# A spectral layer on 32x64 tokens with X(k) and X(-k) side by side, and an FFN on normalised rows in 64-row PE tiles

## The chip, the cores and the metric

The kernel runs on one core of one Trainium2 chip. The metric is the time of one execution on the device in microseconds (us), lower is better. A time quoted for a kernel is the median of its runs. The span that a profile shows is the time from the first to the last instruction on the core; it is 1.6 to 2.8 us shorter than the time of the same run in the runs here. Engines are written PE (matrix multiplications), PEld (loading of weights for PE), DVE (vector engine), ACT (scalar engine), POOL, and SP, which here only issues DMAs. A DMA is carried out by 16 DMA engines in packets, the contiguous pieces that the trace records one by one.

## The reference, cut to what matters

The reference applies the same two kinds of layers twice, first A, then B, then A, then B, with the same weights both times. The input has 2048 tokens with 448 features in bf16.

```
def _A_ref(x, w_r, w_i):                       # spectral layer
    X = rfft2(x.astype(float32), axes=(-2, -1))      # 2048 x 225
    X = X * (w_r + 1j * w_i)
    return irfft2(X, s=(S, D)).astype(bfloat16)

def _B_ref(x, w1, b1, w2, b2):                 # FFN: 448 -> 1792 -> 448
    h = einsum("bsd,df->bsf", x, w1) + b1
    r = where(h > 0, h, 0)
    return einsum("bsf,fd->bsd", r * r, w2) + b2

x = A_x
x = x + _A_ref(_layernorm(x), A_w_r, A_w_i)
x = x + _B_ref(_layernorm(x), B_w1, B_b1, B_w2, B_b2)
x = x + _A_ref(_layernorm(x), A_w_r, A_w_i)
x = x + _B_ref(_layernorm(x), B_w1, B_b1, B_w2, B_b2)
```

The complex weights W = w_r + i w_i have 2048 x 225 elements each for the real and the imaginary part. One row, without its first column, is 224 elements, which is 448 bytes in bf16.

## The kernel before

The transform over the 2048 tokens is done in two factors, 16 x 128. The names of the stages, which the profile lets one tell apart by their tiles, are these:

- A: a 16-point transform over token tiles (weights `Fs`).
- TD (layer 1) or TQ (layer 2): the transform over the features (tiles `TD_sb` and `TQ_sb`).
- B: the 128-point transform over the tokens (`G_sb`).
- W: DVE multiplies by the spectral weights.
- Bi: the 128-point inverse (`H_sb`, `HS_sb`).
- TI and AI: the inverse over the features and the last 16 points (`TI_sb`, `FI_sb`), which form the ramp into the FFN.
- h and o: the two products of the FFN, both with `W_sb`.

A real input gives X(k) and X(-k) that belong together, so each block needs the weights of row k and of row -k. The kernel loads both halves of W with all 128 partitions as destination, each row once, and makes the mirrored order of the second half with PE and a permutation matrix J:

```
w_dram = [w.rearrange("(p k) l -> p k l", k=16) for w in (A_w_r, A_w_i)]
for i in range(2):
    dma("sp", Wn[:, i, :, :], w_dram[i][:, 9:16, 1:225])        # 128 partitions
...
    dma("sp", Wp[:, :, 2 * i, :], w_dram[i][:, 1:8, 1:225])     # 128 partitions
...
def w_mirror(p):
    q = _Tile(1)
    for i in range(2):
        mm(q[...], J_sb[:], Wn[:, 1 - i, 7 - p, :], i == 0, i == 1, skip=True)
    evac(Wp[:, p - 1, 1:4:2, :], q[...], EV["M"])
```

The first product of the FFN contracts over 448 features. The kernel pads them to four blocks of 128 rows. The rows are not normalised; the spare rows of the fourth block carry sums of columns of W1 and the bias, with which the mean is corrected, and the factor of the normalisation is applied at the end, in `o_tile`:

```
def h_part(c, fb, t0, t1):
    ...
    for blk in range(4):                       # 4 full passes for 3.5 blocks of features
        mm(q[...], W1_sb[:, blk, fb * P:(fb + 1) * P], yT[:, 4 * c + t0:4 * c + t1, blk, :],
           blk == 0, blk == 3)
    act(hb, q[...], ACT.Relu)
    tt(hb, hb, hb, ALU.mult)
```

A list scheduler in the program fixes the order of all instructions on every engine when the kernel is built. It works from assumed costs and from priorities that stand in a table. In the profile nearly every matmul bears the line of one helper (L530), so groups are told apart by tile names and shapes.

Of the kernel before, what the change touches and what calls it, by code (L numbers as in the profile page):

```python
# [10 lines left out]
P = 128  # L11
S = 2048
# [10 lines left out]
SD_PAIRS = (4, 5, 6, 7)  # L23
H_PAIRS = tuple(p for p in range(1, 8) if p not in SD_PAIRS)

# [9 lines left out]
def make_constants():  # L35
# [3 lines left out]
    comp = np.zeros((16, 16))  # L39
    hi = np.arange(16)  # L40
    comp[0] = 1.0
    comp[1] = np.cos(np.pi * hi)
    for p in range(1, 8):
        comp[2 * p] = np.cos(2 * np.pi * p * hi / 16)
        comp[2 * p + 1] = -np.sin(2 * np.pi * p * hi / 16)
    FA = np.zeros((16, 8, 16, 8))
    for j in range(8):
        FA[:, j, :, j] = comp.T
# [24 lines left out]
    m = np.arange(P)  # L73
    lo = (m % 8) * 16 + m // 8
    k2 = np.arange(P)
    kk = [0, 8, 1, 2, 3, 4, 5, 6, 7]
    G = np.zeros((P, 9, 3, P))
    H = np.zeros((P, 9, 2, 2 * P))
    for i, k1 in enumerate(kk):
        th = 2 * np.pi * lo[:, None] * (k1 + 16 * k2[None, :]) / float(S)  # L80
        G[:, i, 0] = np.cos(th)
        G[:, i, 1] = -np.sin(th)
        G[:, i, 2] = np.sin(th)
        hr = np.cos(th).T
        hm = np.sin(th).T
        if i < 2:
            H[:, i, 0] = np.concatenate([hr, hm], 1)
            H[:, i, 1] = np.concatenate([-hm, hr], 1)
        else:
            a = np.stack([hr.reshape(P, 16, 8), hm.reshape(P, 16, 8)], 2)  # L90
            b = np.stack([-hm.reshape(P, 16, 8), hr.reshape(P, 16, 8)], 2)
            H[:, i, 0] = a.reshape(P, 2 * P)
            H[:, i, 1] = b.reshape(P, 2 * P)
# [9 lines left out]

    HS = np.stack([np.stack([-H[:, p + 1, 1], H[:, p + 1, 0], H[:, p + 1, 1], -H[:, p + 1, 0]], 1) for p in SD_PAIRS], 1)
    H = H[:, [0, 1] + [p + 1 for p in H_PAIRS]]
    return dict(HS=HS, FA=np.concatenate([FA, -FA], 1), FI=np.concatenate([FI, -FI], 1), TD=TD, G=G, H=H, TI=TI, TQ=TQ,
# [4 lines left out]
PR = {'A1': 65800.0, 'A1step': 7500.0, 'TD': [48800.0, -113100.0], 'B': [36300.0, -23900.0], 'W': [76300.0, 35800.0], 'Bi': [21700.0, 28400.0], 'step': [16400.0, 1100.0], 'M': 33500.0, 'aux': -104400.0, 'ramp': [210200.0, 192900.0], 'rstep': [2800.0, 6700.0], 'late': [85200.0, 100700.0], 'lstep': [5400.0, 6200.0], 'TI': [53500.0, 42800.0], 'AI': [44600.0, 400.0], 'h': [57700.0, -6500.0], 'A2': -27100.0, 'xb': 113100.0}  # L111
LOOK = {'act': 0.0, 'dve': 50.0, 'pe': 0.0}
EV = {'A1': ['act'], 'A2': ['act'], 'TD': ['act', 'dve'], 'B': ['act', 'dve'], 'Bi': ['act', 'dve'], 'Bi0': ['act', 'dve'], 'TI': ['act'], 'M': ['act', 'dve'], 'T': ['act', 'dve'], 'XR': ['pool'], 'FS': ['pool'], 'FS2': ['dve']}
SPLIT = (1, 2, 4)
NFLIP = 2
HALVES = True
# [3 lines left out]
class _Op:  # L120
    __slots__ = ("eng", "fn", "deps", "has_dep", "ticket", "is_dma", "dsem", "cost", "lat", "unit", "gdeps", "alt")

    def __init__(self, eng, fn, is_dma, cost, lat):
        self.eng = eng
        self.fn = fn
        self.deps = []
        self.gdeps = []
        self.has_dep = False
        self.ticket = None
        self.is_dma = is_dma  # L130
        self.dsem = None
        self.cost = cost
        self.lat = lat
        self.unit = None
        self.alt = None

# [6 lines left out]
class _Unit:  # L143


    def __init__(self, eng, tile=None):
        self.eng = eng
        self.ops = []
        self.tile = tile
        self.prio = 0.0  # L150
        self.bias = 0.0
        self.seq = 0

# [29 lines left out]
def _pages(ap):  # L183

    if isinstance(ap, _PsAP):
        return [ap.tile]
# [7 lines left out]
    return [(name, int(i)) for i in pg]  # L194


class _Sched:
# [6 lines left out]
    DMA_RATE = 400.0  # L204

    def __init__(self):
# [5 lines left out]
        self.look = dict.fromkeys(self.ENGINES, 0.0)  # L212
        self.warm_fn = None
# [3 lines left out]
        self.warm_share = 0.45  # L217

    def add(self, eng, fn, reads=(), writes=(), is_dma=False, cost=100.0, lat=130.0, unit=None):
# [24 lines left out]
        elif tile is not None and tile.unit is not None:  # L244
            u = tile.unit
        else:
            u = _Unit(eng, tile)
            u.bias = self.bias
            u.seq = len(self.units)
            self.units.append(u)  # L250
            if tile is not None:
                tile.unit = u
# [3 lines left out]
        op.unit = u  # L256
        u.ops.append(op)
        return op

    def schedule(self):  # L260
# [17 lines left out]
        for u in self.units:  # L278
            if u.tile is not None:
                for r in u.tile.readers:  # L280
                    for d in r.gdeps:
                        if d.unit.seq < u.seq:
                            order[d.unit].add(u)
                            npred[u].add(d.unit)
        free = {e: 0.0 for e in self.ENGINES}
# [8 lines left out]

        def enter(u):
            for e in u.ops[0].alt or (u.eng,):
                cand[e].append(u)

        for u in self.units:
            if left[u] == 0:  # L300
                enter(u)
        ready = {}

        def ready_of(u):
            if u not in ready:
                r, off = 0.0, 0.0
                for op in u.ops:
                    for d in op.gdeps:
                        if d.unit is not u:
                            same = d.eng == u.eng and not d.is_dma  # L310
                            r = max(r, done[d] + d.lat + (80.0 if u.eng == "pe" else 0.0) - off)
                    off += op.cost
                ready[u] = r
            return ready[u]
# [11 lines left out]

        total = len(self.units)
        while total:
            choice = None
            for e in self.ENGINES:  # L330
                avail, starts = {}, []
                for u in cand[e]:
                    r = ready_of(u)
                    if u.tile is not None:
                        if u.tile.n not in avail:
                            avail[u.tile.n] = pick_banks(u.tile.n, free[e])
                        if avail[u.tile.n] is None:
                            continue
                        r = max(r, avail[u.tile.n][0])
                    starts.append((max(r, free[e]), u))  # L340
                if starts:

                    t0 = min(s for s, u in starts) + self.look[e]
                    best = min(((-u.prio, u.seq, s, u) for s, u in starts if s <= t0), key=lambda k: k[:2])
                    key = (best[2], best[0], best[1])
                    if choice is None or key < choice[0]:
                        choice = (key, best[3], e)
            assert choice is not None, "no unit can run"
            start, u, e = choice[0][0], choice[1], choice[2]
            if e == "pe":  # L350

                while self.warm_fn is not None:
                    gap = start - free["pe"]
                    recent = sum(min(b, free["pe"]) - max(a, free["pe"] - 3400.0) for a, b in used[-60:]
                                 if b > free["pe"] - 3400.0)
                    cold = free["pe"] < self.cold_until
                    unit = 430.0 if cold else 216.0
                    if gap < unit + (150.0 if cold or recent < self.warm_share * 3400.0 else 700.0):
# [16 lines left out]
                if u.tile is not None and start < free["pe"]:  # L375
                    start = free["pe"]
            for a in u.ops[0].alt or (e,):
                cand[a].remove(u)
            if u.ops[0].alt:
# [4 lines left out]
            if u.tile is not None:  # L384
                b = pick_banks(u.tile.n, start)[1]
                u.tile.bank = b
                for i in range(b, b + u.tile.n):
                    old = bank_user[i]
                    if old is not None and old is not u.tile:
# [3 lines left out]
                    bank_user[i] = u.tile  # L393
            t = start
            for op in u.ops:
                t += op.cost
# [5 lines left out]
                for a in (op.gdeps if e != "pe" else ()):  # L402
                    if a.eng == "pe" and a.unit.tile is not None:
                        for i in range(a.unit.tile.bank, a.unit.tile.bank + a.unit.tile.n):
# [44 lines left out]
def bass_interleave_layers__spectral_gfnet__dense_activation_squared_relu__prompt_kernel(nc, A_x, A_w_r, A_w_i, B_x, B_w1, B_b1, B_w2, B_b2, out):  # L449
# [6 lines left out]
    with ExitStack() as es:  # L456
# [7 lines left out]
        x_sb = sb("x_sb", [P, NT, 4 * P])  # L464
        xin = sb("xin", [P, NT, D])
        XA = sb("XA", [P, 2, 2, 16, P])
# [3 lines left out]
        Z = arena[:, 7168 * 2:7168 * 2 + 32 * 256].rearrange("p (c l) -> p c l", c=32)  # L470
# [4 lines left out]
        VT = sb("VT", [P, 2, 2, NT, 16, 8])  # L475
# [3 lines left out]
        Wn = yT[:].rearrange("p a b c -> p (a b c)")[:, 0:2 * 7 * LW].rearrange("p (r k l) -> p r k l", r=2, k=7)  # L479
        Wt = sb("Wt", [P, 32, LW])  # L480
        TD_sb = sb("TD_sb", [P, 2, 2, LW])
        G_sb = sb("G_sb", [P, 9, 3, P])
        H_sb = sb("H_sb", [P, 2 + len(H_PAIRS), 2, 2 * P])
        HS_sb = sb("HS_sb", [P, len(SD_PAIRS), 4, 2 * P])
# [8 lines left out]
        W1_sb = sb("W1_sb", [P, 4, FF])  # L493
        W2_sb = sb("W2_sb", [P, FB, D])
# [4 lines left out]
        r2 = rstd[:, :, 4:8]  # L499
# [13 lines left out]
        def dma(eng, o, i, transpose=False):  # L513
            reads = [i] if i.tensor.name in onchip else []
            writes = [o] if o.tensor.name in onchip else []
# [6 lines left out]
            else:  # L522
# [3 lines left out]
                sch.add(eng, fn, reads, writes, is_dma=True, cost=60.0 if eng == "sp" else 100.0,  # L526
                        lat=2.0 * n / sch.DMA_RATE)

        def mm(o, lhsT, rhs, start, stop, skip=False):
# [603 lines left out]
```

## Time and profile before

The first three runs had a median of 291.64 us (288.81 to 291.81). With the fourth run, made beside the changed kernel, the median is 290.23 us.

These are the lines of part 1 (busy time), part 2 (the span in 40 slices) and part 4 (the chain of waits by engine) of the page of the kernel before. In part 2 a digit is the busy share of a slice in tenths; PEclk is the clock granted to PE in tenths; a slice is 7.15 us.

```profile
PE 270.9 (95%) x1769; PEld 163.6 (57%) x1771; DVE 210.4 (74%) x738; ACT 175.4 (61%) x375; POOL 13.3 (5%) x28
...
PE   7799999799999999999996989889999999999996
...
PEclk9999999999999999999999999999999999999999
DMA  7999400010321000110000000020221300020001
GB/s 259 337 376 373 100 0 1 21 19 2 73 40 38 0 0 2 37 38 2 0 0 2 0 1 2 0 40 0 71 71 37 76 32 32 0 71 32 0 18 48
...
PE 81%; DVE 13%; DMA 2%; issue 1%; ACT 1%; POOL 1%; SPq 0%; DVEq 0%; POOLq 0%
```

PE is busy for 95% of the span, never at a reduced clock, and the chain that ended last goes through PE for 81% of its length. DMA is busy mainly in the first five slices (later digits are at most 3).

These are lines of part 5, the groups of instructions: line, engine, operation, tiles, shapes, count, then busy us and mean ns of one, then idle time before them and what ended it.

```profile
L530 PE MATMUL ps<-yT,W_sb 128*128 128x512 bf16 (+1 forms) x560 | 98.6, 337 | 1.3 <-ACT VT L913 0.7
L549 ACT ACTIVATE arena<-ps 128x512 bf16<-128x512 f32 (+1 forms) x140 | 69.3, 514 | 43.4 <-PE ps L530 41.3
```

The first line is the h product: 560 full passes, 98.6 us. The second is its Relu.

The table of stretches gives for each stage its length, the busy time of PE, PEld, DVE, ACT and POOL with the number of instructions, the clock, the busy share of the DMA engines (it is the time of all packet records over 16 engines, so it passes 1 where more than 16 packets are under way at once) and GB/s. The stages were cut where the timeline of PE shows a new tile. The four rows are spectral layer 1, FFN 1, spectral layer 2 and FFN 2.

```profile
19.22:46.45 27.23, 26.19 (x183) 17.19 (x183) 23.86 (x55) 23.12 (x40) 0.00 (x0) 1.00 0.47 152
...
54.02:150.40 96.38, 96.38 (x600) 55.71 (x600) 80.94 (x332) 56.16 (x132) 0.00 (x0) 1.00 0.10 20
...
154.53:180.51 25.98, 24.31 (x164) 15.17 (x166) 21.52 (x49) 21.31 (x35) 0.00 (x0) 1.00 0.00 1
...
188.28:286.00 97.72, 94.33 (x558) 53.43 (x558) 55.86 (x185) 46.42 (x105) 0.00 (x0) 1.00 0.16 39
```

The FFNs are bound by PE alone. The spectral layers are nearly balanced between PE, DVE and ACT. The same table in 4 us steps shows what the DMA engines moved at the start of spectral layer 1:

```profile
20.00:24.00 4.00, 4.00 (x37) 3.26 (x35) 3.50 (x9) 3.20 (x6) 0.00 (x0) 1.00 1.05 343
24.00:28.00 4.00, 4.00 (x32) 2.81 (x29) 3.97 (x12) 3.82 (x8) 0.00 (x0) 1.00 1.06 377
```

Here the queue holds the rest of the weights and constants, and 343 to 377 GB/s go through at a full DMA share while PE is busy all the time. The timeline of PE shows one 512-column chunk of h in FFN 1 (start, length, engine, tiles, count):

```profile
123.88 12.25 PE L530 MATMUL ps<-yT,W_sb 128*128 128x512 bf16 x56
```

### The profile page before, as it was taken

The numbers are of one execution on the slowest core, as the hardware profiler recorded it, in microseconds if no ns is written. First come the engines' busy times: TensorE is split into PE (matmuls) and PEld (weight loads), VectorE is DVE, ScalarE is ACT, GpSimd is POOL, SyncE is SP. The second block draws the span as 40 slices with busy tenths as digits, with TensorE's granted clock in tenths as the row PEclk, the third lists the DMA queues.
The fourth block names the chain that finished last, engine by engine and source line by source line (L and its number), as shares of the span: only waits on it lengthen the run. The fifth ranks groups of instructions, "written<-read, shape, count | busy, mean of one in ns | idle before, by whom it ended". The sixth has DMA issues, their size and how long they took to land.

```text
span 286.0 us, 5056 instructions
## 1 busy us (share of the span) xinstructions
PE 270.9 (95%) x1769; PEld 163.6 (57%) x1771; DVE 210.4 (74%) x738; ACT 175.4 (61%) x375; POOL 13.3 (5%) x28
## 2 busy tenths in 40 slices
PE   7799999799999999999996989889999999999996
PEld 2697746687544455544575554767754454454454
DVE  4959995998998469995695898599589723553432
ACT  2698977998466745347326997796649603623610
POOL 4930000000000000000000000000000000000000
PEclk9999999999999999999999999999999999999999
DMA  7999400010321000110000000020221300020001
GB/s 259 337 376 373 100 0 1 21 19 2 73 40 38 0 0 2 37 38 2 0 0 2 0 1 2 0 40 0 71 71 37 76 32 32 0 71 32 0 18 48
DMA packets 26156, 16.11 MB, mean 56 GB/s; under 512 B 19954, under 2 KB 24786, under 8 KB 26004
## 3 DMA queue, kind: packets, MB, share of 16 engines
q1 hardware_dynamic: 25700, 15.04, 18.8%
q10 hardware_dynamic: 432, 0.75, 0.8%
q8 instruction: 14, 0.23, 0.3%
q14 instruction: 10, 0.08, 0.1%
HBM read 10.29 MB, written 1.84 MB: 42 GB/s over the span
## 4 chain that ended last, share of the span: by engine, by line
PE 81%; DVE 13%; DMA 2%; issue 1%; ACT 1%; POOL 1%; SPq 0%; DVEq 0%; POOLq 0%
PE ps L530 81%; DVE tmp L574 6%; DMA xin<-in_A_x_dram 2%; DVE arena L574 1%; DVE x_sb L889 1%; DVE yT L556 1%; POOL VT L556 1%; DVE x_sb L961 1%; DVE VT L556 1%; DVE st L674 0%; DVE VT L574 0%; DVE arena L556 0%; ACT XA L555 0%; ACT arena L555 0%; ACT VT L913 0%
## 5 line engine op out<-in xcount | busy, mean ns | idle before, releaser
L530 PE MATMUL ps<-yT,W_sb 128*128 128x512 bf16 (+1 forms) x560 | 98.6, 337 | 1.3 <-ACT VT L913 0.7
L549 ACT ACTIVATE arena<-ps 128x512 bf16<-128x512 f32 (+1 forms) x140 | 69.3, 514 | 43.4 <-PE ps L530 41.3
L530 PE MATMUL ps<-W_sb,arena 128*128 128x448 bf16 (+1 forms) x476 | 88.1, 341 | 0.0
L530 PEld LDWEIGHTS ps<-yT,W_sb 128*128 128x128 bf16 x560 | 54.2, 98 | 44.1 <-issue 0.9
L574 DVE TENSOR_TENSOR arena<-arena 128x512 bf16<-128x512 bf16 (+1 forms) x140 | 50.4, 370 | 27.8 <-ACT arena L549 25.0
L530 PEld LDWEIGHTS ps<-W_sb,arena 128*128 128x128 bf16 x476 | 46.0, 98 | 35.6
L961 DVE SCALAR_TENSOR_TENSOR x_sb<-ps,rstd,arena 128x448 bf16<-128x448 f32 (+1 forms) x34 | 22.2, 654 | 26.0 <-PE ps L530 25.8
L555 ACT ACTIVATE arena<-ps 128x896 bf16<-128x896 f32 (+1 forms) x36 | 25.0, 759 | 3.2 <-PE ps L530 2.7
L549 ACT ACTIVATE mv<-mv,epst 128x2 f32<-128x2 f32 (+1 forms) x38 | 10.9, 296 | 23.1 <-DVE mv L675 18.1
L913 ACT ACTIVATE VT<-x_sb 128x448 bf16<-128x448 bf16 x32 | 18.2, 569 | 8.1 <-DVE x_sb L889 7.5
L555 ACT ACTIVATE XA<-ps 128x512 bf16<-128x512 f32 x32 | 17.6, 600 | 7.7 <-PE ps L530 7.6
L555 ACT ACTIVATE VT<-ps 128x512 bf16<-128x512 f32 (+1 forms) x32 | 17.5, 582 | 5.3 <-PE ps L530 5.1
L555 ACT ACTIVATE tmp<-ps 128x896 bf16<-128x896 f32 (+1 forms) x18 | 14.7, 829 | 4.5 <-PE ps L530 4.5
L574 DVE TENSOR_TENSOR tmp<-tmp,Wt 128x896 bf16<-128x896 bf16 (+1 forms) x32 | 16.0, 567 | 0.0
L530 PE MATMUL ps<-HS_sb,arena 128*128 128x512 bf16 x62 | 14.2, 379 | 0.6 <-DVE arena L574 0.4
L530 PE MATMUL ps<-arena,G_sb 128*128 128x448 bf16 (+1 forms) x72 | 14.1, 334 | 0.4 <-ACT arena L555 0.3
L530 PE MATMUL ps<-TI_sb,VT 112*128 112x112 bf16 (+1 forms) x128 | 10.1, 224 | 2.3 <-ACT tmp L555 0.9
L889 DVE SCALAR_TENSOR_TENSOR x_sb<-ps,x_sb 128x448 bf16<-128x448 f32 x16 | 9.6, 622 | 2.9 <-PE ps L530 2.7
L674 DVE BATCH_NORM_STATS2 st<-xin 128x6 f32<-128x448 bf16 x16 | 9.5, 606 | 2.5 <-DMA xin<-in_A_x_dram 2.5
L530 PEld LDWEIGHTS ps<-TI_sb,VT 112*128 112x128 bf16 x128 | 8.3, 97 | 4.4 <-DVE VT L556 1.4
L530 PEld LDWEIGHTS ps<-HS_sb,arena 128*128 128x128 bf16 x64 | 5.9, 98 | 8.3 <-DVE arena L574 1.7
L674 DVE BATCH_NORM_STATS2 st<-x_sb 128x6 f32<-128x448 bf16 (+1 forms) x17 | 10.1, 597 | 0.2
(73 smaller groups left out, 279.4 us busy)
## 6 DMA issues: line engine op xcount, KB each, us to landing
out_dram<-x_sb SPq DMA_DIRECT2D x15, 112.0 KB, 1.7
W_sb<-in_B_w_dram SPq DMA_DIRECT2D x1, 1568.0 KB, 14.4
W_sb<-in_B_w_dram SPq DMA_DIRECT2D x1, 1344.0 KB, 10.1
HS_sb<-c_HS SPq DMA_DIRECT2D x1, 1024.0 KB, 6.0
xin<-in_A_x_dram SPq DMA_DIRECT2D x2, 448.0 KB, 6.0
G_sb<-c_G SPq DMA_DIRECT2D x1, 672.0 KB
xin<-in_A_x_dram ACTq DMA_DIRECT2D x1, 448.0 KB, 5.3
yT<-in_A_w_r_dram SPq DMA_DIRECT2D x1, 392.0 KB, 8.4
```

Of the source, the lines that this page charges most:

```text
L530: sch.add("pe", lambda e: e.matmul(_res(o), lhsT, rhs, start=start, stop=stop, skip_group_check=skip), [lhsT, rhs], [o], cost=max(_free(rh ...
L549: sch.add("act", lambda e: e.activation(o, _res(i), func, **kw), rd, [o], cost=c)
L555: op = sch.add(engs[0], lambda e: e.activation(o, _res(i), ACT.Copy) if h[0].eng == "act" else e.tensor_copy(o, _res(i)), [i], [o], cost=c ...
L556: e.tensor_copy(o, _res(i)), [i], [o], cost=c[engs[0]], unit=unit)
L574: sch.add(eng, lambda e: e.tensor_tensor(o, _res(a), b, op), [a, b], [o], cost=_free(o) / rate + 69.0)
L674: small(lambda e, si=si, xi=xi: e.bn_stats(si, xi), [xi], [si], _free(xi) / 0.96 + 69.0)
L889: small(lambda e, xx=xx, xi=xi, r=r, i=i: e.scalar_tensor_tensor(out=xx, in0=_res(r), scalar=1.0, in1=xi, op0=ALU.mult, op1=ALU.add, accum ...
L913: sch.add("act", lambda e, i=i, o=o, x=x: e.activation(o, x, ACT.Square, accum_out=sd[:, i, 1:2]), [x], [o, sd[:, i, 1:2]], cost=560.0)
L961: small(lambda e: e.scalar_tensor_tensor(out=o, in0=_res(i), scalar=r2[:, t, 0:1], in1=xb[:, t, d0:d1], op0=ALU.mult, op1=ALU.add), [i, r2 ...
```

## The change

Four things are changed together.

1. The token transform is split 32 x 64. A block p then has X(k) and X(-k) side by side in the columns of one tile, the real parts in partitions 0 to 63 and the imaginary parts in partitions 64 to 127. The sums that the mirror needed are now plain column ranges, and Bi costs fewer columns. In exchange W is needed in two arrangements: once with w_r in partitions 0 to 63 and w_i in 64 to 127 (`Was`, in the buffer `x_sb`, in layer 2 in `xin`), and once exchanged (`Wb`, in the buffer `yT`). The rows for -k come from a copy of the second half of W that is reversed in DRAM (`Wrev`).
2. The rows are normalised before the FFN, so only 448 rows of features remain, with no correction rows. The h product runs in 64-row tiles of PE: two half passes on the lower and the upper 64 rows side by side, 7 half passes per feature block in place of 4 full ones. Relu takes the bias as an operand.
3. The mirrors and the corrections go.
4. Every stage and block has its own priority in the scheduler.

The core of the diff, with cuts marked:

```
-        Wn = yT[:]...   Wt = sb("Wt", [P, 32, LW])
-        G_sb = sb("G_sb", [P, 9, 3, P])
-        H_sb = sb("H_sb", [P, 2 + len(H_PAIRS), 2, 2 * P])
-        HS_sb = sb("HS_sb", [P, len(SD_PAIRS), 4, 2 * P])
+        G_sb = sb("G_sb", [P, NP, 2, 192])            # NP = 16
+        H_sb = sb("H_sb", [P, NP, 2, 256])
...
+        Wrev = [nc.dram_tensor(f"Wrev{i}", (16, 64, LW), BF16, kind="Internal").ap() for i in range(2)]
+        for i in range(2):
+            dma("sp", Wrev[i], (A_w_r, A_w_i)[i].rearrange("(q k) l -> k q l", k=32)[16:32, ::-1, 1:225], ...)
...
-        for i in range(2):
-            dma("sp", Wn[:, i, :, :], w_dram[i][:, 9:16, 1:225])
-        ...
+        def load_W(W, f, p0, p1):
+            for i in range(2):
+                rows, w = slice(64 * (i ^ f), 64 * (i ^ f) + 64), w_dram[i]
+                dma("sp", W[rows, p0:p1, 0, :], w[:, p0:p1, 1:225])
+                if p0 == 0:
+                    dma("sp", W[rows, 0:1, 1, :], w[:, 16:17, 1:225])
+            for i in range(2):
+                rows = slice(64 * (i ^ f), 64 * (i ^ f) + 64)
+                r, p = Wrev[i].rearrange("k r l -> r k l"), max(p0, 1)
+                dma("sp", W[rows, p:p1, 1, :], r[:, 16 - p:16 - p1:-1, :], reads=[f"Wrev{i}"])
+        for p0, p1 in RANGES:                          # (0, 4), (4, 10), (10, 16)
+            dma("sp", G_sb[:, p0:p1], dc["G"][:, p0:p1])
+            load_W(Was[0], 0, p0, p1)
+            load_W(Wb, 1, p0, p1)
+            dma("sp", H_sb[:, p0:p1], dc["H"][:, p0:p1])
...
-        def h_part(c, fb, t0, t1):    ... for blk in range(4): mm(... W1_sb[:, blk, ...] ...)
+            def both(u, *runs):
+                for n in range(len(runs[0][2])):
+                    for k, rows, blks in runs:
+                        ... mm(qs[k][...], W1_sb[rows, blk, f], y[rows, :, blk, :], ..., half=True, unit=u)
+            ...
+                both(u, (2 * m, LO, (0, 1, 2, 3)), (2 * m + 1, UP, (0, 1, 2, 3)))
+                    both(u, (2 * j + 1, LO, (0, 1, 3)), (2 * j, UP, (0, 2, 3)))
```

## The prediction

The sum came to -18.8 us (-5 - 3.5 - 12.3 + 2.5 - 0.5, "about -19"). Terms are cut from the text, where marked: the +2.5, the middle of an allowance of 2 to 3 us for about 20 changes between row tiles and full passes, and a named risk that goes with it. The allowance was the author's guess; no run had shown such a cost. It is still contained in the 272.0 us, in the "about -19" and in the lengths given for the FFNs.

> **What bounds it now.** The page shows PE busy 270.9 of 286.0 us (95%), PEclk 9 in every slice; the chain of waits is 81% PE, 13% DVE. Stages by the timeline of PE: start to 9.3; first A to 19.2; spectral layer 1 to 46.5; ramp to 54.0; FFN 1 to 150.4; gap to 154.5; spectral layer 2 to 180.5; ramp to 188.3; FFN 2. The table of stretches shows PE busy all 96.4 us of FFN 1 and 94.3 of 97.7 us of FFN 2. The spectral layers are nearly balanced: layer 1 (27.2 us) PE 26.2, DVE 23.9, ACT 23.1; layer 2 (26.0 us) PE 24.3, DVE 21.5, ACT 21.3; there the chain goes through DVE's multiplications by W.
>
> **What changes, costed from the trace.** In dense runs PE starts a 512-column matmul every 216-218 ns, 256 every 109, 224 about 95, 128 (A2) about 56, 112 (TI) about 50.
> 1. FFN h: 448 rows cost 4 passes now (560 matmuls, 98.6 us). With 64-row tiles they cost 7 half passes, paired, so 3.5: -12.3 us if two row tiles really run together. [...] Relu now takes a bias operand (perhaps 90 ns more on ACT: one-element sqrts take 294 ns with bias, 203 without), but 596+90 stays under PE's new 756 ns a block.
> 2. Inverse stage (Bi): 24,576 columns a layer become 16,384 (18,432 in layer 2), as 128 or 144 matmuls of 128 columns: 10.4 us to about 7.1 and 8.0. B keeps its columns (6.1 us). Mirrors (14 matmuls of 224, 1.3 us) and the sums for the weight correction (16 of 448, 3.0 us) go.
> 3. DVE: the W stage shrinks from about 19 us a layer to 16.8 and 15.7 (four 896-column operations of 535 ns per two blocks); 7 mirror evictions (about 0.56 each) go. Normalising adds 32 tensor_scalars, perhaps 0.35 each; corrections of similar size go.
> 4. DMA: W needs twice the bytes in layer 1 (3.7 MB), reversed through DRAM (0.9 MB), again 3.7 MB for layer 2, under FFN 1. At the 340-375 GB/s of the first slices layer 1's 11 MB land by 31-33 us, in order of need: tight, not binding.
>
> **Sum.** Layer 1: PE needs 19.4 us, DVE and ACT about 20 each, so 27.2 becomes 22 (-5). Layer 2: -3.5. FFNs: -12.3[...]. First A stage: -0.5. Ramps: 0. About -19 in all, nearly all on the critical path.
>
> **Predicted 272.0 us, 263 to 280** (8 in 10). Faster by over 2%: 0.94; within 2%: 0.045; slower: 0.015.
>
> **What would show it.** PE busy near 250; h matmuls in pairs, starts a pair about 216-220 ns apart, 10.6 us instead of 12.1 for a 512-column chunk; Bi about 56 ns a matmul; PEclk still 9; FFN 1 near 91 us, FFN 2 near 92; spectral layers near 22; no waits of DVE on W's DMA over 1 us.
>
> **What would make it wrong.** Row tiles overlapping less than 1.75 times (h then gains nothing); weight loads limiting 64-row pairs at 256 columns or Bi at 128; runs of four columns slowing writes to PSUM in Bi, as layer 2's stride-2 outputs seem to (about 98 ns for 112 columns); [...]W's DMA late in layer 1.

## The result, and the profile after

The changed kernel takes 278.65 us (276.85 to 279.06, four runs) against 290.23 us, and its outputs are correct. A ratio is the mean time of one kernel's fast runs over that of the other's in the same rounds, so it is not quite the ratio of the medians: it is 0.9598, with a 95% interval of 0.9539 to 0.9657. The change is 4% faster. The prediction said 6.7% faster (272.0 of 291.64) with a range of 263 to 280, so the sign and the range hold, while most of the expected gain of some 19 us is there and a part of it isn't.

The same parts of the page, now of the changed kernel (a slice is 6.92 us):

```profile
PE 257.8 (93%) x2385; PEld 168.5 (61%) x2385; DVE 206.8 (75%) x686; ACT 176.5 (64%) x366; POOL 9.6 (3%) x23
...
PE   6699586999998999999999999899999999999995
...
PEclk9999978999999999999999999999999999999999
DMA  7969999702223424202240400002332700111001
GB/s 239 307 143 267 295 244 335 253 2 47 62 48 68 86 40 100 60 0 56 53 93 3 98 2 4 0 2 41 21 75 58 144 3 4 46 50 36 0 22 46
...
PE 67%; ACT 7%; DVE 7%; DMA 1%; issue 1%; DVEq 0%; ACTq 0%
```

In slices 3 to 7 the digits of DMA are as full as before or fuller (6 to 9), yet GB/s is 143, 267, 295, 244, 335 where the kernel before had 376, 373 and was nearly done. In slices 5 to 7 PE is busy only 5, 8 and 6 tenths, and in slices 6 and 7 its clock is reduced. The two groups of the FFN:

```profile
L600 ACT ACTIVATE arena<-ps,b1T 128x512 bf16<-128x512 f32 (+1 forms) x140 | 73.5, 611 | 30.8 <-PE ps L577 30.6
L577 PE MATMUL ps<-yT,W_sb 64*128 64x512 bf16 (+1 forms) x980 | 86.1, 333 | 1.2 <-DMA yT<-xin 0.8
```

The h product fell from 98.6 to 86.1 us of busy time. Here are the four stages again from the table of stretches, in the same order:

```profile
20.07:52.26 32.19, 25.26 (x264) 22.55 (x265) 19.96 (x38) 20.54 (x30) 0.00 (x0) 0.89 1.10 292
...
60.34:150.70 90.36, 89.53 (x785) 51.83 (x785) 83.25 (x325) 57.04 (x133) 0.00 (x0) 1.00 0.27 55
...
154.61:177.25 22.64, 21.56 (x275) 20.39 (x276) 18.31 (x35) 19.97 (x31) 0.00 (x0) 1.00 0.04 9
...
185.84:276.80 90.96, 87.77 (x748) 50.03 (x748) 55.76 (x179) 45.64 (x101) 0.00 (x0) 1.00 0.19 42
```

FFN 1, FFN 2 and spectral layer 2 are 6.0, 6.8 and 3.3 us shorter. Spectral layer 1 is 5.0 us longer, at a granted clock of 0.89 and a DMA share above 1 for its whole length. Laid beside the prediction, in us:

| stage | before | predicted | after | difference after - before |
|---|---|---|---|---|
| start to first TD | 19.2 | 18.7 | 20.1 | +0.9 |
| spectral layer 1 | 27.2 | 22 | 32.2 | +5.0 |
| ramp 1 | 7.6 | 7.6 | 8.1 | +0.5 |
| FFN 1 | 96.4 | 91 | 90.4 | -6.0 |
| gap (FFN 1 to layer 2) | 4.1 | 4.1 | 3.9 | -0.2 |
| spectral layer 2 | 26.0 | 22.5 | 22.6 | -3.3 |
| ramp 2 | 7.8 | 7.8 | 8.6 | +0.8 |
| FFN 2 | 97.7 | 92 | 91.0 | -6.8 |
| span | 286.0 | about 267 | 276.8 | -9.2 |

(The column of predictions is read from the text of the prediction; its parts add to 266. The span of 286.0 belongs to one of the fastest runs of the kernel before, 288.8 us, so the spans differ by 9.2 us and the medians by 11.6.)

Without spectral layer 1 the stages were predicted to give 14 us and gave 14.2. Layer 1 was to give 5 and cost 5. The whole miss of about 10 us lies there. The timeline of PE in this stage shows how the time was lost:

```profile
29.35 2.46 PE L577 MATMUL ps<-TD_sb,XA 128*128 128x224 bf16 x24
35.46 4.14 PE L577 MATMUL ps<-arena,G_sb 128*128 128x224 bf16 x24 [3.65 <-DMA G_sb<-c_G]
39.43 2.84 PE L577 MATMUL ps<-H_sb,arena 128*128 128x128 bf16 x48
42.11 1.46 PE L1104 MATMUL ps<-ones 128*128 128x512 bf16 x6
45.54 0.23 PE L577 MATMUL ps<-H_sb,arena 128*128 128x128 bf16 x1 [1.97 <-DVE arena L635]
46.07 5.30 PE L577 MATMUL ps<-H_sb,arena 128*128 128x128 bf16 x63 [0.30 <-DVE arena L635]
```

PE waits 3.65 us for the last part of G. After this pause the 24 matmuls of 224 columns take 4.14 us, while 24 of the same width (first line) take 2.46. The granted clock is 0.50 from 35.8 us on for 3.4 us (0.60 in the mean from 36 to 40 us, see the table below). Later PE waits only 1.97 us for DVE, and from 46.1 us the clock is again 0.50 for 3.4 us, so that the last 63 matmuls take 5.30 us (3.69 in e12 below). A pause of 2.54 us in e11 below brought no such fall. So in these runs the shorter pause of 1.97 us was followed by a reduced clock and the longer one of 2.54 us was not; what decides it is not shown. The `ones` matmuls are fillers that the scheduler puts where it expects PE to idle. The table of waits says what DVE and PE waited for on DMAs (us in total, times, longest):

```profile
DVE tmp L635 <- DMA yT<-Wrev: 5.8, 2, 2.9
...
PE ps L577 <- DMA G_sb<-c_G: 4.2, 2, 3.6
...
DVE tmp L635 <- DMA x_sb<-Wrev: 2.2, 2, 1.4
```

So 8.0 us of waits of DVE and 4.2 us of PE are on W and G. The table of stretches in 4 us steps:

```profile
20.00:24.00 4.00, 3.93 (x42) 3.96 (x43) 2.06 (x5) 2.56 (x4) 0.00 (x0) 1.00 1.01 291
24.00:28.00 4.00, 3.45 (x39) 3.20 (x37) 2.87 (x7) 3.52 (x6) 0.00 (x0) 1.00 1.21 229
28.00:32.00 4.00, 3.81 (x46) 3.56 (x43) 0.77 (x2) 3.83 (x7) 0.00 (x0) 1.00 1.09 286
32.00:36.00 4.00, 0.54 (x5) 0.53 (x6) 4.00 (x8) 0.89 (x2) 0.00 (x0) 0.98 1.12 285
36.00:40.00 4.00, 4.00 (x32) 3.38 (x31) 2.46 (x5) 2.20 (x3) 0.00 (x0) 0.60 1.20 235
```

The DMA engines are busy all the time and move 229 to 291 GB/s, where the kernel before had moved 343 and 377. Before 20 us they were not even busy: the timeline of SP shows that issuing a W DMA takes about 0.62 us, for 28 KB and for 168 KB alike when nothing else holds SP up, and SP issues them one by one (two in each line). Parts of G, which go to 128 partitions in large packets, took 0.43 us here, the parts of H that follow W 0.68 to 0.72, so the number of partitions alone doesn't decide it. Lines of that timeline:

```profile
12.34 1.25 SPq L572 DMA_DIRECT2D x_sb<-Wrev  x2
13.63 1.27 SPq L572 DMA_DIRECT2D yT<-in_A_w_r_dram  x2
14.94 1.25 SPq L572 DMA_DIRECT2D yT<-in_A_w_i_dram  x2
```

From 12 to 16 and from 16 to 20 us the engines moved 182 and 134 GB/s at shares of 0.77 and 0.62.

### The profile page after: what moved, and what is told of

It is laid out like the page before. It is cut to its first block, busy times and chain, and to the rows that moved or that the text cites. A ratio compares the mean times of both kernels' runs of the same rounds, so it can differ in the third digit from the quotient of the medians.

```text
span 276.8 us, 6385 instructions
## 1 busy us (share of the span) xinstructions
PE 257.8 (93%) x2385; PEld 168.5 (61%) x2385; DVE 206.8 (75%) x686; ACT 176.5 (64%) x366; POOL 9.6 (3%) x23
## 4 chain that ended last, share of the span: by engine, by line
PE 67%; ACT 7%; DVE 7%; DMA 1%; issue 1%; DVEq 0%; ACTq 0%
PE ps L577 67%; ACT VT L617 3%; ACT tmp L617 2%; ACT arena L617 2%; DMA yT<-xin 1%; DVE tmp L635 1%; DVE x_sb L912 1%; DVE x_sb L910 1%; ACT yT L617 1%; DVE arena L635 1%; DVE xin L644 1%; DVE XA L618 0%; DVE st L928 0%; DVE VT L635 0%; DVE x_sb L1009 0%
## 5 line engine op out<-in xcount | busy, mean ns | idle before, releaser
L600 ACT ACTIVATE arena<-ps,b1T 128x512 bf16<-128x512 f32 (+1 forms) x140 | 73.5, 611 | 30.8 <-PE ps L577 30.6
L577 PE MATMUL ps<-yT,W_sb 64*128 64x512 bf16 (+1 forms) x980 | 86.1, 333 | 1.2 <-DMA yT<-xin 0.8
L577 PEld LDWEIGHTS ps<-yT,W_sb 64*128 64x128 bf16 x980 | 49.9, 94 | 37.0 <-issue 1.8
L1009 DVE TENSOR_TENSOR x_sb<-ps,arena 128x448 bf16<-128x448 f32 (+1 forms) x34 | 20.1, 595 | 23.7 <-PE ps L577 23.4
L577 PE MATMUL ps<-H_sb,arena 128*128 128x128 bf16 x272 | 18.8, 230 | 2.6 <-DVE arena L635 2.6
L577 PE MATMUL ps<-arena,G_sb 128*128 128x224 bf16 x128 | 16.2, 280 | 4.2 <-DMA G_sb<-c_G 4.2
L577 PEld LDWEIGHTS ps<-H_sb,arena 128*128 128x128 bf16 x272 | 17.5, 104 | 3.5 <-DVE arena L635 3.4
L617 ACT ACTIVATE VT<-ps 128x512 bf16<-128x512 f32 x29 | 15.6, 636 | 4.5 <-PE ps L577 4.5
L577 PEld LDWEIGHTS ps<-arena,G_sb 128*128 128x128 bf16 x128 | 13.0, 107 | 5.5 <-DMA G_sb<-c_G 4.7
L635 DVE TENSOR_TENSOR arena<-tmp 128x896 bf16<-128x896 bf16 (+1 forms) x30 | 16.2, 586 | 0.1
```

The source lines that it names most:

```text
L577: op = sch.add("pe", lambda e: e.matmul(_res(o), lhsT, rhs, start=start, stop=stop, skip_group_check=skip), [lhsT, rhs], [o], cost=max(_fr ...
L600: sch.add("act", lambda e: e.activation(o, _res(i), func, **kw), rd, [o], cost=c)
L617: op = sch.add("act", lambda e: e.activation(o, _res(i), ACT.Copy) if h[0].eng == "act" else e.tensor_copy(o, _res(i)), [i], [o], cost=c[" ...
L635: sch.add(eng, lambda e: e.tensor_tensor(o, _res(a), b, op), [a, b], [o], cost=_free(o) / rate + 69.0)
L1009: sch.add("dve", lambda e: e.tensor_tensor(o, _res(i), xb[:, t, d0:d1], ALU.add), [i, xb[:, t, d0:d1]], [o], cost=(d1 - d0) / 0.96 + 69.0)
```

## The experiments

Theories at the outset. T1: W's DMAs are the cause of the loss in layer 1, since W comes late. Rivals within it: the small packets of 448 bytes, the number of issues, the detour through DRAM, and the order in which G is asked for. (That the partitions that a DMA writes might matter was taken up only after the first eight runs.) T2: the layer 1 stage itself is slower (for instance its new schedule), and the DMA waits only fill time. For the FFN: that the 64-row tiles are the whole gain there. All experiments start from the changed kernel and were timed in three rounds against the kernel before, on the same chip as it within each group (e1 to e4 and e5 to e8 on chip 7, e9 and e10 on chip 4, e11 and e12 on chip 6). Where the text compares with the changed kernel, its 278.65 us are meant, which were not measured in those rounds: the comparison goes through the kernel before, whose median was 290.0 to 290.1 us in all the groups.

| run | outputs | median us | ratio to before | 95% | layer 1, us |
|---|---|---|---|---|---|
| (changed kernel) | correct | 278.65 | 0.9598 | 0.9539 to 0.9657 | 32.2 |
| e1_full_rows | correct | 292.05 | 1.0059 | 0.9998 to 1.0120 | 33.2 |
| e2_free_w | wrong | 268.64 | 0.9249 | 0.9190 to 0.9308 | 22.3 |
| e3_big_packets | wrong | 274.70 | 0.9475 | 0.9403 to 0.9546 | 28.3 |
| e4_g_first | correct | 277.18 (fast runs) | 0.9546 | 0.9471 to 0.9621 | profile not used |
| e5_few_wrev | wrong | 268.34 | 0.9241 | 0.9190 to 0.9292 | 22.3 |
| e6_swap | correct | 276.40 | 0.9517 | 0.9446 to 0.9588 | 30.5 |
| e7_swap_order | correct | 276.24 | 0.9513 | 0.9463 to 0.9563 | 30.2 |
| e8_swap_wide | correct | 279.50 | 0.9619 | 0.9561 to 0.9676 | 35.4 |
| e9_alternate | correct | 273.71 | 0.9434 | 0.9388 to 0.9479 | 25.5 |
| e10_alternate_swap | correct | 269.19 | 0.9284 | 0.9245 to 0.9322 | 24.1 |
| e11_two_halves | wrong | 276.81 | 0.9542 | 0.9489 to 0.9596 | 31.3 |
| e12_two_alternate | wrong | 268.69 | 0.9272 | 0.9211 to 0.9334 | 22.3 |

Where the outputs are wrong, W's buffers are filled with other numbers, so the shapes and the work of the engines stay and only the DMAs differ.

### e1_full_rows: the row tiles undone

```
+        memset(W1_sb[0:64, 2, :], 0.0, eng="pool")     # rows that two blocks share
-            ... both(...) in 64-row tiles
+            for k in range(FB):
+                for blk in range(4):
+                    mm(qs[k][...], W1_sb[:, blk, k * P:(k + 1) * P], y[:, :, blk, :], blk == 0, blk == 3)
+                h_out(c, k, t0, t1, qs[k])
```

> The changed kernel with the 64-row tiles alone undone: every h column block takes four 128-row passes again (rows 192 to 255, which the new layout holds twice, are zeroed in one copy of W1), result still right. My theory: pairs of row tiles start 3 ns apart in the trace, a pair every 216 ns, and 12 changes of mode cost about 95 ns each, so the tiles are worth 12.3 - 1.1 = 11 us: time of the changed kernel plus 10 to 12 us, about 289. Rival: the tiles' gain is partly given back elsewhere (evictions by ACT become the limit of the h stage), so undoing them costs 6 us or less.

It took 292.05 us, 13.4 more than the changed kernel. The h matmuls were busy 98.5 us, as in the kernel before (98.6). FFN 1 was 97.2 and FFN 2 96.3 us long, against 90.4 and 91.0: 12.2 us together. Of these, 2.1 us are nine filler matmuls in FFN 1 that the changed kernel does not have there, so the tiles themselves are worth about 10 us in the FFNs, near the 11 us of the theory; the total of 13.4 went past its 10 to 12 us. The rest is 1.0 us in layer 1 and 0.3 in the second ramp. So without row tiles nothing would be left of the gain: the other parts of the change together were worth about nothing, because what layer 2 gained was lost in layer 1.

### e2_free_w: W from one contiguous DMA a range

```
-        Wrev = [...] and its two DMAs
-            (six to eight DMAs of W per range)
+            h = dc["H"].rearrange("p k s l -> p (k s l)")
+            n = 2 * LW
+            dma("sp", W.rearrange("p k s l -> p (k s l)")[:, p0 * n:p1 * n], h[:, p0 * n:p1 * n])
```

> The changed kernel with wrong data on purpose: each range of each copy of W comes as one DMA of the same bytes out of a constant, contiguous per partition, and the reversal through DRAM is gone. Theory 1 (spectral layer 1 takes 32.2 us instead of layer 2's 22.6 because W, G and H land late): layer 1 falls to 22.5 to 25 us, no wait on DMA over 1 us in it, clock 1.00, time 8 to 10 us under the changed kernel. Theory 2 (layer 1 is slow by itself: longer chains[...]): it falls by less than 3 us.

With the same number of bytes in W's buffers, but one DMA to 128 partitions with large packets per copy and range, layer 1 takes 22.3 us and the whole 268.64 us. That is the 22 us that the prediction gave layer 1. T2 falls: the compute of the new layer 1 is as short as foreseen (layer 2, whose W is loaded under FFN 1, takes 22.6 us in the changed kernel as well). The loss is in how W is loaded.

### e3_big_packets: the same number and size of DMAs, with contiguous packets

```
-                dma("sp", W[rows, p0:p1, 0, :], w[:, p0:p1, 1:225])
+                dma("sp", Wf[rows, p0 * n:m * n], h[rows, p0 * n:m * n])
...            (likewise for the other W DMAs; Wrev stays and is waited for)
```

> The changed kernel with wrong data on purpose: as many DMAs of W as in the changed kernel, of the same sizes and on the same queue, the reversal through DRAM still made, but each partition's share is one contiguous piece instead of pieces of 448 bytes. If the 448-byte packets are what is slow (28 to 37 ns each, 194 to 256 GB/s over 16 engines, against 350 to 370 for large ones): layer 1 falls by 4 to 7 us. If the issue on SP is (0.62 us for each W DMA, whatever its size, back to back from 5 to 30 us): less than 2 us.

It took 274.70 us, 4.0 less than the changed kernel and 6.1 more than e2. The packets of 448 bytes are thus a part, not the main part (the interval just touches that of the changed kernel, 0.9546 and 0.9539, but no run of the one overlaps with the other's). PE still waited 3.77 us for the last of G. The table of stretches from 12 to 20 us:

```profile
12.00:16.00 4.00, 3.87 (x36) 3.47 (x37) 3.37 (x18) 3.53 (x10) 2.84 (x7) 1.00 0.75 185
16.00:20.00 4.00, 3.57 (x30) 2.52 (x27) 2.77 (x9) 3.53 (x8) 0.67 (x2) 1.00 0.69 153
```

With large packets and as many DMAs the DMA engines are about as idle here as in the changed kernel (182 and 134 GB/s at 0.77 and 0.62), so small packets are not what keeps the rate low before 20 us.

### e4_g_first: all of G ahead of W

```
+        for p0, p1 in RANGES:
             dma("sp", G_sb[:, p0:p1], dc["G"][:, p0:p1])
         for p0, p1 in RANGES:
             load_W(...)
```

> The changed kernel with all of G issued before W and H; nothing else moved, result right. In the changed kernel PE waits 3.6 us for the last range of G and DVE 5.8 + 2.2 us for W. If the order of G behind W and H is the cause: 3 to 5 us less. If the total supply is: the wait on G goes, the waits on W grow, the time stays within 1.5 us.

The three fast runs had a median of 277.18 us, 1.5 less; the intervals overlap, so no difference is shown, and certainly not the 3 to 5 us that the order of G would have been worth. That PE now waits for W's work in its place, as was expected, is not shown, because no fast run was profiled. A fourth run took 381.18 us at a granted clock of 0.66. The profile fell on it and nothing is read from it.

### e5_few_wrev: e2, with the detour through DRAM kept

```
         (as e2, but the two Wrev DMAs are still issued; nothing waits for them)
```

> Wrong data on purpose: as e2 (each range of each copy of W is one large DMA of the same bytes), but the two DMAs that reverse half of W through DRAM are still made at their place, though nothing waits for them. e2 took 10.0 us off the changed kernel, e3 (large packets, as many issues, reversal kept) 4.0. The remaining 6 us are the reversal or the 22 issues more. If the reversal: 272 to 275 us. If the issues: 268 to 270 us.

It took 268.34 us (e2: 268.64). The reversal itself, 0.9 MB written to DRAM in packets of 448 bytes, costs nothing that shows. (Nothing waits for it here. In the changed kernel SP doesn't either: it issues the first rows that come from `Wrev` at 12.34 us, straight after the DMA before.) Of the two explanations foreseen this left the number of issues; but e5 also writes 128 partitions with each DMA, and e11 and e12 show later that this is what counts.

### e6_swap and e7_swap_order: the second copy from the first, on the chip

In e6 only the first copy comes from DRAM. The exchanged copy is made of it by DMAs from partitions to partitions:

```
-            load_W(Wb, 1, p0, p1)
+                for i in range(2):
+                    dma("sp", Wb[64 * (1 - i):64 * (2 - i), p0:p1], Was[0][64 * i:64 * i + 64, p0:p1])
```

> The changed kernel, right result: in layer 1 the second copy of W is made by DMA from the first one on chip (the partition halves exchanged, packets of 1.8 to 2.7 KB) in place of a second read from DRAM in 448-byte pieces; H and the exchange come after the next range's loads. Bytes the same, 4,096 fewer small packets[...], 10 fewer issues. If packets and issues both count: 3 to 5 us less than the changed kernel, 274 to 276. If the wait of each exchange for its source to land costs as much: no gain.

e7 adds to this a better order: small loads on ACT's queue, small constants first.

> As e6, and the two small loads of W are issued by ACT before its first work, and the three small constants are issued ahead of the reversal through DRAM (their issue took 3.1 us behind it). Right result. If issue on SP early in the span is part of the cause: 1 to 2 us less than e6. If not: the same within 1 us.

They took 276.40 and 276.24 us, 2.3 and 2.4 less than the changed kernel, with intervals that overlap with its own. The 28 W DMAs of layer 1 had become 20, half of W's small packets were gone, and still most of the loss stayed: from 19 to 28 us e6 moved 265 GB/s at a share of 1.10, and DVE waited 7.4 us for the exchanged copy. The finer order of e7 brought nothing measurable; with it PE waited 2.0 us for the rows of b1. By then the number of small packets and of issues had been tried without much result. What the slow kernels had in common, unlike e2 and e5, was that each W DMA wrote 64 neighbouring partitions.

### e8_swap_wide: reversal in pieces of 900 bytes

```
-  Wrev (16, 64, 224), read row by row of 448 bytes
+  Wrev (64, 16 * 225), the reversal in pieces of 900 bytes (two rows)
```

> As e7, with the reversal through DRAM in pieces of 900 bytes in place of 448 (whole rows, two at a time), 1,024 in place of 2,048. Right result. If the reversal's small packets are a cost: 1 to 2 us less than e7. It may run on fewer engines and then land later: then it is slower than e7.

This was a miss. It took 279.50 us, 3.3 more than e7; layer 1 was 35.4 us long, and DVE waited 11.5 us for the exchanged copy. SP could issue the second DMA from the reversed copy only at 15.1 us (12.6 in e7), and later waited 6.5 us (4.6 in e7) for the last rows to land before it could issue their exchange. The expectation had named a reason, that the larger pieces go to fewer engines. The packet records fit it: never more than 12 packets of 900 bytes were under way at once, mostly 8 to 10, against mostly 16 to 22 of 448 bytes in the changed kernel's reversal. No run varied this alone.

### e9_alternate: real and imaginary parts on alternate partitions

G's columns and H's rows are permuted so that w_r lies in the even partitions and w_i in the odd ones. All DMAs of W keep their number, size and packets.

```
+    alt = np.arange(P).reshape(2, 64).T.reshape(P)
-            G[:, p, q] = np.concatenate([...], 1)                       # 192 wide
+            G[:, p, q] = np.concatenate([...[:, alt], ...[:, alt]], 1)  # 256 wide
-                H[:, p, q] = np.concatenate([b, -b if q == 0 else b])
+                H[:, p, q] = np.concatenate([b, -b if q == 0 else b])[alt]
-                dma("sp", W[64 * (i ^ f):64 * (i ^ f) + 64, ...], src[i])
+                dma("sp", W[(i ^ f)::2, ...], src[i])
```

> The changed kernel, right result: w_r and w_i land on alternate partitions instead of partitions 0 to 63 and 64 to 127 (columns of G and rows of H permuted on the host; G then needs 256 columns a block in place of 192, 0.5 MB more). Number, size, order and packets of the W DMAs stay. In e3 a 2,688-byte packet to 64 partitions took 183 ns, in e5 a 5,376-byte packet to 128 partitions 207 ns, and H's 6,144-byte packets 350 ns in the changed kernel against 234 to 255 in e5. [...] If that halved rate is a main cause: large packets fall back to 180 to 260 ns, W's to 25 to 30 ns, and the time falls by 3 to 6 us, to 272.5 to 275.5. If the number of issues is: no gain, or 1 us lost to the larger G.

(The halved rate is that of the numbers before it: 2,688 bytes in 183 ns against 5,376 in 207.)

It took 273.71 us, 4.9 less than the changed kernel, although G has a third more bytes. Layer 1 fell to 25.5 us. In the records of DMA packets from 20 to 36 us a packet of 448 bytes took 25 to 26 ns (means of 4 us windows), against 31 to 38 ns in the changed kernel, and 25 to 29 in the kernel before from 8 to 20 us.

### e10_alternate_swap: e9 with the second copy made on the chip

```
-            load_W(Wb, 1, p0, p1)
+                    dma("sp", Wb[1 - i::2, p0:p1], Was[0][i::2, p0:p1])
+            (two small W loads on ACT's queue)
```

> e9 and the on-chip second copy of e6 together (10 issues and 4,096 small packets fewer), and the two small loads of W issued by ACT; right result. If [...]packets and issues each cost something: 269 to 272 us, near e2 and e5.[...]

The outputs are correct and it took 269.19 us (268.93 to 270.19), ratio 0.9284 (0.9245 to 0.9322). This is the fastest correct kernel. Its interval lies wholly below that of the changed kernel, and by the medians it is 3.4% faster than it. Its spectral layer 1 in the table of stretches:

```profile
19.55:43.66 24.11, 22.84 (x266) 20.34 (x267) 19.70 (x38) 19.98 (x30) 0.00 (x0) 1.00 1.04 367
```

And the timeline of PE in the same kernel, at the place where the changed kernel stood still:

```profile
28.10 2.46 PE L592 MATMUL ps<-TD_sb,XA 128*128 128x224 bf16 x24
30.40 2.46 PE L592 MATMUL ps<-arena,G_sb 128*128 128x224 bf16 x24
32.70 0.61 PE L592 MATMUL ps<-H_sb,arena 128*128 128x128 bf16 x8
```

367 GB/s against 292, no wait for G, and the 24 matmuls of G take 2.46 us, because the clock was never reduced (1.00). With alternate partitions, the smaller number of issues and small packets is worth 4.5 us (e9 to e10); with halves it was worth 2.3 (changed kernel to e6), which is not clear of noise.

### e11_two_halves and e12_two_alternate: the partitions alone

In e9 the wins might still have come from some other difference. These two kernels differ in one line. Both fetch W as two large-packet DMAs per range and copy, both have the 256-wide G and neither waits for the reversal. One writes partitions 0 to 63 and 64 to 127, the other every second partition. In their traces the order of the instructions is the same on every engine.

```
e11:  prev = dma("sp", V[64 * i:64 * i + 64, p0 * n:p1 * n], h[64 * i:64 * i + 64, p0 * n:p1 * n], ...)
e12:  prev = dma("sp", V[i::2,               p0 * n:p1 * n], h[64 * i:64 * i + 64, p0 * n:p1 * n], ...)
```

> Wrong data on purpose, for a clean pair with e12: as e5 (large contiguous packets, nothing waits for the reversal), but each range of each copy of W comes as two DMAs of 64 partitions, 0 to 63 and 64 to 127, in place of one of 128; G as large as in e9. If the half of the partitions is what slows: W's packets take 350 ns and more in place of e5's 207 to 215, the rate from 16 to 32 us of the span falls from e5's 350 to 420 GB/s to under 300, and the time is 2 to 5 us over e12. If not: as e12 within 1 us.

> Wrong data on purpose: e11 with one difference, the two DMAs go to every second partition, even and odd. [...]packets of W back at 200 to 220 ns, 268 to 270 us, as e5 with its single DMAs, which also shows that six issues more cost nothing. If issues decide: as e11.

(The first case is that the partitions decide.)

The halves took 276.81 us and the alternate partitions 268.69, 8.1 us apart. The table of stretches in 4 us steps, of e11:

```profile
20.00:24.00 4.00, 3.67 (x39) 3.70 (x40) 1.80 (x4) 2.38 (x5) 0.00 (x0) 1.00 1.03 240
24.00:28.00 4.00, 4.00 (x50) 4.00 (x48) 3.67 (x9) 4.00 (x6) 0.00 (x0) 1.00 1.01 281
28.00:32.00 4.00, 3.35 (x38) 3.09 (x34) 3.64 (x7) 3.96 (x6) 0.00 (x0) 1.00 1.04 317
```

The same steps in e12:

```profile
20.00:24.00 4.00, 3.63 (x38) 3.66 (x39) 1.76 (x4) 2.38 (x5) 0.00 (x0) 1.00 1.02 413
24.00:28.00 4.00, 4.00 (x50) 4.00 (x49) 3.89 (x10) 4.00 (x6) 0.00 (x0) 1.00 1.01 419
28.00:32.00 4.00, 4.00 (x47) 4.00 (x45) 4.00 (x8) 3.96 (x6) 0.00 (x0) 1.00 1.03 384
```

The DMA engines are equally busy (the share is 1.01 to 1.04 in both), and each packet takes longer in e11. Not all of the 8.1 us is waiting: after a pause of 3.97 us PE in e11 ran at a clock of 0.50 for 6.8 us, and its last 63 matmuls of H took 5.90 us (3.69 in e12). From the records of DMA packets in the trace, mean duration of one by size, in ns:

| packets | destination | e11_two_halves | e12_two_alternate |
|---|---|---|---|
| W, 5,376 bytes | 64 partitions | 345 to 387 | 206 to 214 |
| H, 6,144 bytes | 128 partitions | 327 to 429 where it follows W | 234 to 289 |

(The values are means of 4 us windows from 16 to 40 us that have at least 20 such packets. One window of e11, 28 to 32 us, has 261 ns for H, and one from 16 to 20 has 240.) With W in halves a packet takes 1.7 times as long, and the packets of H to all partitions that share the time with them are slowed as well.

The runs show that the partitions decide: with the same number, sizes and sources of DMAs and the same order of instructions, the halves took 8.1 us more. What goes with the partition number that causes it, no run shows. In the windows of e11 that hold nearly only W (20 to 24 and 32 to 36 us) 240 and 244 GB/s were moved; e12 moved 413 from 20 to 24 us. e2 with one DMA took 268.64 us and e12 with two DMAs to alternate partitions 268.69, as much as one (e2 ran on another chip and with the narrower G, so this pair is less exact than e11 and e12). The split costs nothing that shows here; the half does.

### What did not come to a run

Loading the reversed rows from W directly into SBUF, without the detour, was built in three forms. None compiled, because the outermost dimension of the access had a negative step. e5 shows that little was to be had there as long as nothing waits for the detour.

## Why the prediction was right or wrong

The sign, the range and the mechanism of the gain were right. One step was wrong, and it hid about half of the gain.

1. **Row tiles (item 1): right.** Predicted -12.3 us for h, with an allowance against it for changes between row tiles and full passes (the +2.5 us above). Measured 98.6 to 86.1 us of busy time (-12.5). The timeline of PE in the changed kernel has a 512-column chunk of h in FFN 1 as

```profile
126.06 10.75 PE L577 MATMUL ps<-yT,W_sb 64*128 64x512 bf16 x98
```

   where 56 full passes took 12.25 us before: 98 half passes are 49 pairs, at 219 ns a pair, and 10.6 us had been predicted. In the trace the two of a pair of 512 columns start 3 or 4 ns apart, or about 20. There are 12 changes between row tiles and full passes (not 20), and in the nine that no other wait covers the next matmul starts about 95 ns (92 to 97) later than in a dense run, so about 1.1 us for all 12. With the 2.5 us allowed, this explains most of why FFN 1 and FFN 2 came out 0.6 and 1.0 us below the prediction. Relu with a bias took 685 ns in place of 596 at 512 columns (+89; predicted +90) and limited nothing, as ACT still idled 30.6 us before it. e1 closes it: without the tiles 13.4 us are lost, 2.1 of them to fillers.
2. **Inverse stage (item 2): right.** In layer 2 the matmuls of 128 columns come about 56 ns apart in dense runs (predicted 56); runs of four columns in PSUM slowed nothing.
3. **DVE (item 3): right where it could be seen.** In layer 2 DVE was busy 18.3 us (21.5 before), and the layer took 22.6 us for the 22.5 predicted. The 32 normalisations took 407 ns each, 0.35 us predicted.
4. **DMA (item 4): wrong, and this is the step that failed.** "At the 340-375 GB/s of the first slices layer 1's 11 MB land by 31-33 us, in order of need: tight, not binding." The bytes were counted correctly. The rate was carried over from DMAs that wrote 128 partitions to DMAs that write 64 neighbouring ones. The changed kernel moved 229 to 291 GB/s from 20 to 36 us, the last range of H was issued at 36.4 us, DVE waited 8.0 us for W and PE 4.2 us for G, and PE then ran at a reduced clock for a while ("PEclk still 9" was wrong in two slices, after pauses of 3.65 and 1.97 us). Layer 1 was mis-sized by 10 us: predicted -5, measured +5. The line `slice(64 * (i ^ f), ...)` in the diff showed the partitions. The prediction did list "W's DMA late in layer 1" among what would make it wrong, with too little weight.
   - Shown: with the partitions as the only difference, 8.1 us (e11 and e12). With alternate partitions in the real kernel, 4.9 us (e9), and 4.5 more when the second copy is made on the chip (e10).
   - Also shown: large packets alone give 4.0 us (e3), the traffic of the detour through DRAM costs nothing (e5), and G's order nothing that can be told apart (e4).
   - Supported, though no run varied it alone: that the cost of issuing on SP (0.62 us a DMA) sets the low rate from 12 to 20 us. With as many W DMAs and large packets e3 moved only 185 and 153 GB/s there, while e11, with 12 W DMAs to the same halves, moved 280 and 364 (e11 also doesn't wait for the reversal and has a larger G). By itself this low rate doesn't decide the time: e11 took 276.81 us and e3 274.70.
5. **Ramps and start: 0 and -0.5 predicted, +1.3 and +0.9 measured.** PE was busy 257.8 us (near 250 predicted); of this, fillers make 12.0 us (40 matmuls, 6.4 us before), and some matmuls ran at the reduced clock. This was not studied further.

The total of 278.65 us was inside the range since the other errors were small: the parts other than layer 1 were predicted to give 14 us and gave 14.2. There was luck in it too: an error of 10 us is more than the 8 us from 272.0 to the upper end of the range. The 272.0 was counted from 291.64 us, while the trace that the stages were costed from was of a run of 288.8; counted from that run, the same gain and the same 8 us would have ended near 277, and missed. e10 makes the test of this: with the loading mended the profiled span is 267.4 us, where the prediction had its spans at about 267.

Left open: what makes two DMAs to 64 neighbouring partitions slower than two to every second one; whether the fewer packets under way are why e8 was slower; how much of the 1.8 us by which e10's layer 1 is still longer than e2's comes from its last exchange (SP waits 3.4 us for the rows that it copies, and DVE then 1.2 us for the copy); when a pause of PE lowers its clock; the slightly longer ramps and start; and the very slow run of e4.

## What to carry to other kernels

When a change moves a tensor to another arrangement, ask which partitions each DMA writes before a measured rate is carried over: two DMAs to partitions 0 to 63 and 64 to 127 were 8.1 us slower in this kernel than the same two to even and odd partitions, and here the arrangement could be chosen freely, since it only permuted constants (and made G a third larger). Keep the same stage elsewhere as a control: layer 2, whose weights were loaded long before, said at once that the compute was as short as predicted and that the loading was the fault. A DMA that came late cost twice here: PE waited 3.65 us for it, and then ran at a clock of 0.50 for 3.4 us, so that 24 matmuls took 4.14 instead of 2.46 us.
